# Two attention and MLP layers on one core: Q moved by strided DMAs, stored sums kept in place, and a reordered last stage

## The chip, the core and the metric

The kernel runs on one core of a Trainium2 chip. A core has five engines that run side by side, each through its own list of instructions in order: TensorE (PE, the matmuls; its weight loads are listed as PEld), VectorE (DVE), ScalarE (ACT), GpSimd (POOL) and SyncE (SP, which here only issues DMAs). They wait for each other by semaphores. SBUF is the memory of 128 partitions that all of them use; PSUM is where TensorE puts its results, in 8 banks of 128 x 512 floats. Sixteen DMA engines carry what SP, ScalarE and GpSimd issue.

The metric is the device time of one execution in microseconds (us); smaller is better. Profiles are of one execution, with times counted from the start of its span. Line numbers such as L1420 are lines of the kernel file before the change.

## The reference

```python
def _A_ref(x, wqkv, wo):                      # attention, H = 32 heads of Dh = 16
    qkv = (x @ wqkv).reshape(B, S, 3, H, Dh).transpose(2, 0, 3, 1, 4)
    q, k, v = qkv[0], qkv[1], qkv[2]
    scores = einsum("bhqd,bhkd->bhqk", q, k) * (Dh ** -0.5)
    p = softmax(scores, axis=-1)
    o = einsum("bhqk,bhkd->bhqd", p, v)
    return o.transpose(0, 2, 1, 3).reshape(B, S, D) @ wo
def _B_ref(x, w1, w2):
    return max(x @ w1, 0) @ w2
x = A_x                                       # 1 x 2048 x 512, bf16
x = x + _A_ref(layernorm(x), A_wqkv, A_wo)    # wqkv 512 x 1536, wo 512 x 512
x = x + _B_ref(layernorm(x), B_w1, B_w2)      # w1 512 x 1792, w2 1792 x 512
x = x + _A_ref(layernorm(x), A_wqkv, A_wo)
x = x + _B_ref(layernorm(x), B_w1, B_w2)
```

The same weights serve both layers. The exponentials of the scores are the large part: 2 layers x 32 heads x 2048 x 2048.

## The kernel before, in words

**Tiles and stages.** Queries are cut in four chunks of 512 columns (the second layer's last two chunks are cut further, into three of 256 and two of 128: `chunks`), keys in 16 blocks of 128. The heads are worked in groups: a *run* is one chunk of queries and eight heads (index T, four per layer), and has two *segments*, e = 0 and 1, of four heads each, whose scores stand on four groups of 32 partitions. There are 56 runs, counted through both layers. A *block* is the score of one head's 128 keys against 512 queries (or two or four blocks of keys against 256 or 128 queries). There are 4096 blocks.

**Slots.** The main loop (L1280 to L1446) goes by *slots*. In a slot TensorE scores three blocks into the three banks of one of two PSUM tiles (`ps_s`, L1411), and ScalarE makes one instruction of exponentials over them (L1420). In some slots VectorE takes the third block; ScalarE then has two. Two such blocks make a *pair*, which VectorE turns into exponentials by a chain of its own: `lin` (L1105, from PSUM), two bit masks (`step`, L1146), two products (`cube`, L1157 and L1161), and a scaling (L1158) where V was not scaled beforehand. The result stands as a sum of three terms, so TensorE takes three matmuls with V (L998) for such a block and one for the others. These sums gather in `ps_o`; the ones column of `vaug` gives the softmax denominator in the same matmuls.

**Q.** A run's two heads of a pair share 32 partitions, and the scores of one must not see the other's Q. So Q is kept twice, with the other head's rows set to zero: `q_masked` (L681) has VectorE read the projection from PSUM once per head and multiply by a column of zeros and scales, into `qbuf`, two buffers used by turns. Within the 32 partitions head e = 0 has the first 16, e = 1 the last.

**What ends a segment.** `finish_segment` copies `ps_o` to a buffer `u` (L912), or adds a stored part to it (L910), sends the denominators through small DMAs to a column shape (`c`, L917), inverts them (L939), sends them back (L940), spreads them (a DMA by GpSimd, L942, or a shuffle on VectorE, L952) into a buffer `r` and multiplies (`ot`, L928). There are three `u` and three `r`, taken by turns: segment n waits until segment n - 3 has multiplied. At the start of each layer the keys aren't all there, so partial sums are *stored* (L889, L891) in memory that is free then (`acc0`, in the place of `ht`; `acc`, in that of the first layer's keys and values), and added in the last part.

**The order.** It is written out by the program itself before it is built: a plan keeps a clock for TensorE, VectorE and ScalarE with assumed costs, and puts the projections, the MLP and the layernorms as pieces between the scores where the clocks leave room. `mark` notes when something is made, with a lag where a DMA makes it; `run_until` forces what is missing. VectorE takes a block of a segment up to two segments ahead if that segment's Q is marked and its chain will be done in time. So a change of an assumed cost moves instructions throughout. On the chip each engine follows the order so written, and waits at semaphores.

**Start.** SP and ScalarE load x and the weights; `wqkv` comes in three parts of 512 KB (K on SP; Q, then V on ScalarE), then the rest of x, `wo` and `w2` on SP. The first layernorm, the transposes on TensorE, and the first K, Q and V follow. The later chunks' normed rows are transposed by DMAs on SP (L573); GpSimd does the layernorm's small steps (`ln_seed`, L492 to L500).

**End.** The last chunk has 128 rows. After the last exponential the MLP pieces that are left are run (`run_all`, L1451), among them five groups of the first MLP projection of the chunk before. Then come the last rows' output projection (L1473), layernorm with VectorE steps for the root (`ln_root`), the second projection of the chunk before (`half_part`), and the last rows' MLP, in which the second projection follows the first by one block of 128 features.

Of the kernel before, what the change touches and what calls it, by code (L numbers as in the profile page):

```python
# [19 lines left out]
EPS = 1e-5  # L20
# [5 lines left out]
def kernel(  # L26
# [56 lines left out]
    RSTD_LAG = 4000.0  # L83
    AHEAD = (8.0, 8.0)
# [11 lines left out]
    FULL = 3  # L96

# [11 lines left out]
    wqkv = sb([P, NDC, 3 * D], BF16, "wqkv")  # L109
# [69 lines left out]
    def load_w(engine, a):  # L179
        engine.dma_start(out=wqkv[:, :, a : a + D], in_=wq_src[:, :, a : a + D])  # L180
# [8 lines left out]
    load_w(nc.sync, D)  # L189
    load_w(nc.scalar, 0)  # L190
    load_x(nc.sync, (4, 5, 6, 7))
    load_w(nc.scalar, 2 * D)
    load_x(nc.sync, range(8, NTT))
    nc.sync.dma_start(out=wo[:], in_=A_wo[:, :].rearrange("(c p) f -> p c f", p=P))
    nc.sync.dma_start(out=w2[:], in_=B_w2[:, :].rearrange("(c p) f -> p c f", p=P))

    make_identity(nc, ident[:])
    for kb in range(NKB):
        nc.gpsimd.memset(vaug[0][kb][:, :, DH : DH + 2], 1.0)
    for kb in range(NKB - TPC):  # L200
        nc.gpsimd.memset(vaug[1][kb][:, :, DH : DH + 2], 1.0)


# [6 lines left out]
    def bank():  # L210
        if ending[0]:
            bank_no[0] += 1
            return (ps_f[:], ps_s[0][:, 0, :], ps_s[1][:, 0, :])[bank_no[0] % 3]
# [313 lines left out]

    def ln_apply(tag, tt, i):
        n = ln_n(tag)
        nc.vector.tensor_scalar(  # L530
# [5 lines left out]
    def ln_transpose(tag, i, b=None, at_bank=None):  # L536
        pt = bank().bitcast(BF16) if b is None else b
        for c in range(NDC):
# [3 lines left out]
            if wide[0]:  # L542
                uses(ins, in_bank[0] if b is None else at_bank)
        mark(("xT", tag, i), "pe")
# [5 lines left out]
    def ln_rows(tag, tt, n, i):  # L550
# [10 lines left out]
        if i == n - 1:  # L561
# [6 lines left out]
            def apply(k):  # L568
# [3 lines left out]
                _, l, j = tag  # L572
                nc.sync.dma_start_transpose(  # L573
# [53 lines left out]
    def k_mms(T, j):  # L627
        return [(wqkv[:, c, D + T * P : D + (T + 1) * P], xnT[j][:, c, :]) for c in range(NDC)]
# [11 lines left out]
    def v_mms(kb):  # L640
        j, i = divmod(kb, TPC)
        return [
            (xnT[j][:, c, i * P : (i + 1) * P], wqkv[:, c, 2 * D : 3 * D]) for c in range(NDC)
# [30 lines left out]
    def q_mms(l, j, T):  # L674
        xj, a, w = columns(l, j)
        return [
            (wqkv[:, c, T * P : (T + 1) * P], xnT[xj][:, c, a : a + w]) for c in range(NDC)
# [9 lines left out]
    def q_group(n, l, j, T):  # L687
        xj, _, w = columns(l, j)
        cost = 90 + 2.09 * w

        def fin(b):
            q_masked(n, b, w)
            mark(("q", n))
# [186 lines left out]
    sums_wait = [0]  # L880

    def finish_segment(sg, last):
# [16 lines left out]
        if n >= NU:  # L899
            run_until(("m", n - NU))  # L900
        u, r, c = ubuf[n % NU], rbuf[n % NU], cbuf[n % NU]
# [281 lines left out]
    for e in range(2):  # L1183
# [4 lines left out]
        )  # L1188
        nc.vector.tensor_scalar(
            out=qmask[:, e : e + 1], in0=mask[e], scalar1=SCALE * LOG2E * UNIT, scalar2=None,  # L1190
# [26 lines left out]
    uses(nc.scalar.copy(out=ktp[0][0][0][:], in_=b), in_bank[0])  # L1217
    mark(("k", 0, 0, 0))
# [355 lines left out]
```

## Time and profile before

| | |
|---|---|
| median of 9 runs | 1584.86 us (1582.22 to 1592.49) |
| the profiled execution | 1585.49 us, span 1583.5 us |
| exponentials on ScalarE | 669 over three blocks, 696 over two, one over one |
| pairs on VectorE | 348 |
| Q tiles | 56: 36 of 512 columns, 12 of 256, 8 of 128 |
| first exponential starts, last ends | 14.57 and 1560.85 us |

A group's row in the profile gives line, engine, operation, output and inputs, the number of instructions, the busy time in us, the mean of one in ns, and the idle time of its engine just before it with what ended it. Busy times of one engine can overlap where instructions are pipelined. In a timeline a row gives the start, the length, the instruction, and in brackets the idle time before it. The rows of stretches give start and end, then for each engine the busy time and the number of instructions, then the TensorE clock, the share of the DMA engines and GB/s.

### The profile page before, as it was taken

How to read it: one execution, taken by the hardware profiler on the slowest of the kernel's cores; microseconds unless marked ns; L12 is line 12 of the kernel's file. 1: busy time of each engine (PE TensorE's matmuls, PEld its weight loads, DVE VectorE, ACT ScalarE, POOL GpSimd, SP SyncE). 2: the span in 40 equal slices, each digit the busy share in tenths (PEclk: the TensorE clock that was granted, in tenths of full speed). 3: DMA queues.
4: the chain of work that ended last, by engine and by line, in shares of the span. 5: the costliest groups of instructions: out<-in, count | busy, mean ns of one | idle time of the engine just before them, and what ended most of it. 6: DMA issues, size and time to landing. Idle time of an engine off the chain costs nothing.

```text
span 1583.5 us, 48356 instructions
## 1 busy us (share of the span) xinstructions
PE 1434.3 (91%) x21311; PEld 552.9 (35%) x21311; DVE 1502.4 (95%) x2947; ACT 1549.4 (98%) x1387; POOL 95.8 (6%) x243
## 2 busy tenths in 40 slices
PE   8888889999999989999899998888999999999898
PEld 3222223322332222333233223222334444545665
DVE  7899999999999999999899999999999999999885
ACT  6999999999999999999999999999999999999995
POOL 2000001001010010000100000001001000010000
PEclk9999999998999999999999999999999999999999
DMA  7001100111002120120101000000210211212130
GB/s 193 15 2 26 19 9 18 42 26 25 6 18 43 26 29 6 21 53 11 27 2 27 22 2 1 3 4 9 59 21 17 43 33 27 60 26 58 20 73 16
DMA packets 130145, 44.98 MB, mean 28 GB/s; under 512 B 119280, under 2 KB 127216, under 8 KB 129936
## 3 DMA queue, kind: packets, MB, share of 16 engines
q1 hardware_dynamic: 116864, 29.37, 8.9%
q0 software_dynamic: 11728, 11.23, 4.0%
q8 instruction: 166, 2.72, 0.7%
q10 hardware_dynamic: 1344, 1.31, 0.2%
q14 instruction: 43, 0.35, 0.1%
HBM read 24.38 MB, written 2.10 MB: 17 GB/s over the span
## 4 chain that ended last, share of the span: by engine, by line
ACT 79%; PE 11%; DVE 7%; issue 2%; DMA 1%; ACTq 0%; DVEq 0%
ACT e L1420 79%; PE ps_s L1411 4%; PE ps_o L998 3%; PE ps_f L446 3%; DVE lin L1105 2%; DVE step L1146 1%; DVE cube L1161 1%; DVE cube L1157 1%; DMA wqkv<-in_A_wqkv_dram 1%; PE ps_s L1473 1%; DVE ht L744 0%; DVE q L681 0%; DVE ot L928 0%; DVE u L912 0%; DVE x L705 0%
## 5 line engine op out<-in xcount | busy, mean ns | idle before, releaser
L1420 ACT ACTIVATE e<-ps_s 128x1024 bf16<-128x1024 f32 (+1 forms) x1366 | 1540.1, 1358 | 8.4 <-PE ps_s L1411 7.8
L1411 PE MATMUL ps_s<-q,ktp 32*128 32x512 bf16 (+2 forms) x6699 | 609.6, 325 | 111.9 <-ACT e L1420 101.3
L998 PE MATMUL ps_o<-e,vaug 128*32 128x512 bf16 (+2 forms) x4682 | 497.7, 329 | 8.7 <-DVE u L912 2.7
L1105 DVE TENSOR_SCALAR lin<-ps_s 128x512 int16<-128x512 f32 x696 | 474.3, 684 | 25.3 <-PE ps_s L1411 19.7
L1411 PEld LDWEIGHTS <-ktp 32*128 32x128 bf16 x6699 | 208.9, 91 | 560.9 <-issue 411.7
L998 PEld LDWEIGHTS <-vaug 128*32 128x32 bf16 x6644 | 176.4, 95 | 291.8 <-issue 267.0
L1146 DVE TENSOR_SCALAR step<-lin 128x1024 int16<-128x1024 int16 x696 | 272.7, 416 | 2.1 <-PE ps_o L998 1.2
L1157 DVE TENSOR_TENSOR cube<-step 128x1024 f16<-128x1024 bf16 x348 | 235.4, 681 | 1.7 <-PE ps_f L446 0.5
L1161 DVE TENSOR_TENSOR cube<-cube,lin 128x1024 bf16<-128x1024 f16 x348 | 235.5, 678 | 0.0
L998 PE MATMUL ps_o<-step,vaug 128*32 128x512 bf16 (+2 forms) x950 | 160.0, 328 | 0.0
L446 PE MATMUL ps_f<-w,ht 128*32 128x512 bf16 x1680 | 152.0, 381 | 1.2 <-DVE ht L744 0.5
L446 PE MATMUL ps_f<-xnT,w 128*32 128x512 bf16 (+2 forms) x2080 | 148.2, 341 | 4.7 <-DVE ht L744 3.1
L998 PE MATMUL ps_o<-cube,vthird 128*32 128x512 bf16 (+2 forms) x888 | 143.9, 327 | 0.0
L998 PE MATMUL ps_o<-lin,vaug 128*32 128x512 bf16 (+2 forms) x950 | 126.1, 328 | 6.1 <-DVE u L912 3.7
L446 PE MATMUL ps_f<-xnT,wqkv 128*32 128x512 bf16 (+2 forms) x1376 | 107.8, 351 | 5.4 <-DVE ht L744 1.1
L942 POOL DMA_DIRECT2D r<-u x53 | 39.4, 743 | 1079.9 <-DVE lin L1105 420.0
L446 PE MATMUL ps_f<-wo,ot 128*32 128x512 bf16 x992 | 88.0, 381 | 1.3 <-DVE x L705 1.0
L744 DVE TENSOR_SCALAR ht<-ps_f 128x512 bf16<-128x512 f32 (+1 forms) x107 | 72.7, 679 | 3.3 <-PE ps_f L446 2.7
L446 PEld LDWEIGHTS <-w 128*32 128x32 bf16 x2080 | 59.3, 96 | 34.2 <-issue 17.6
L681 DVE TENSOR_TENSOR q<-ps_f,masks 128x1024 bf16<-128x1024 f32 (+2 forms) x55 | 54.2, 985 | 8.2 <-PE ps_f L446 6.2
L446 PEld LDWEIGHTS <-ht 128*32 128x32 bf16 x1680 | 48.8, 96 | 28.5 <-issue 12.8
L998 PEld LDWEIGHTS <-vthird 128*32 128x32 bf16 x888 | 44.2, 96 | 29.1 <-issue 24.1
(106 smaller groups left out, 609.7 us busy)
## 6 DMA issues: line engine op xcount, KB each, us to landing
w<-in_B_w_dram SPq DMA_DIRECT2D x130, 128.0 KB
r<-u POOLq DMA_DIRECT2D x32, 256.0 KB, 7.4
r<-u POOLq DMA_DIRECT2D x21, 128.0 KB, 4.9
out_dram<-x SPq DMA_DIRECT2D x16, 128.0 KB
x<-in_A_x_dram SPq DMA_DIRECT2D x14, 128.0 KB
w<-in_B_w_dram SPq DMA_DIRECT2D x1, 1792.0 KB
ktp<-in_B_w_dram SPq DMA_DIRECT2D x10, 128.0 KB
wqkv<-in_A_wqkv_dram ACTq DMA_DIRECT2D x2, 512.0 KB
```

Source lines behind the costliest of these rows:

```text
L446: nc.tensor.matmul(out[cols], lhsT[:, cols], rhs, start=i % k == 0, stop=i % k == k - 1, tile_position=(0, 32 * g), skip_group_check=True,)
L681: return nc.vector.tensor_mul(out=qbuf[n % 2][:, :, 0:w], in0=b.rearrange("p (e q) -> p e q", e=1).to_broadcast((P, 2, w)), in1=qmask.rear ...
L744: nc.vector.tensor_scalar(out=out, in0=sums, scalar1=0.0, scalar2=None, op0=ALU.max)
L942: nc.gpsimd.dma_start(out=r[:, 0:width], in_=bass.AP(tensor=sums.tensor, offset=sums.offset, ap=[list(sums.ap[0]), [0, 32], [1, width]],),)
L998: nc.tensor.matmul(ps_o[32 * g : 32 * g + 32, 0 : sg["w"]], values[:, 4 * sg["T"] + g, 2 * e : 2 * e + 32], rhs, start=g not in sg["begun" ...
L1105: first = nc.vector.tensor_scalar(out=lin[which][:, half * QS : (half + 1) * QS], in0=src, scalar1=EXP_BIAS, scalar2=0.0, op0=ALU.add, op1 ...
L1146: nc.vector.tensor_scalar(out=stair, in0=line, scalar1=keep, scalar2=put, op0=ALU.bitwise_and, op1=ALU.bitwise_or,)
L1157: (609, lambda: nc.vector.tensor_mul(out=power, in0=mantissa, in1=mantissa)),
L1161: (609, lambda: nc.vector.tensor_mul(out=power.bitcast(BF16), in0=power, in1=line.bitcast(BF16))),
L1411: nc.tensor.matmul(b[:, a : a + sg["w"]], kt[32 * g : 32 * g + 32, kc : kc + P], qbuf[sg["n"] % 2][32 * g : 32 * g + 32, sg["e"], 0 : sg[" ...
L1420: ex = nc.scalar.activation(out=eb[:, 0 : place[m]], in_=b[:, 0 : place[m]], func=ACTF.Exp, scale=1.0 / (LOG2E * UNIT),)
L1473: uses(nc.tensor.matmul(out, lhsT, rhs, start=first, stop=last), b, needs=needs)
```

## The change

There are four edits, in one program.

1. **Q.** The columns of the K and Q weights are re-sorted, so that within 32 partitions the two heads alternate: e = 0 has the even partitions, e = 1 the odd ones. To do that, the K and Q weights are loaded in eight parts of 128 KB into the memory of `w2`, and copied with a stride into `wkq`, by ScalarE for T = 0 and 1 and by GpSimd for T = 2 and 3. V's weights get their own tile, the load of `w2` is issued after those copies, and `qbuf[1]` is cleared. `q_group` then has two ways. If at least nine slots of work remain before the run and no normed rows wait in `xnbuf[3]`, VectorE evicts Q once, scaled, into `xnbuf[3]`, and two DMAs on SP put the even and odd partitions in place; the plan counts on them 6000 ns later. Else it is the masked copy of before.
2. **Stored sums.** Where a segment has a stored part, the addition writes into the stored part's own memory instead of `u`; all six `u` and `r` buffers become one ring, from which each segment takes what it needs.
3. **Last stage.** VectorE's open tasks are done first, then the output projection and the layernorm of the last rows, and only then what is left of the MLP pieces, on two PSUM banks instead of three. The root is a power on GpSimd. `half_part` is cut in two, with the last rows' transposes between; its result is copied and sent from within the last loop.
4. **Last loop.** The second projection follows the first by three blocks (`LOOK`), not one.

```diff
+    Q_LAG, Q_SLOTS = 6000.0, 9
+    LOOK = 3
-    wqkv = sb([P, NDC, 3 * D], BF16, "wqkv")
+    wkq = sb([P, 2, 4, NDC, P], BF16, "wkq")
+    wv = sb([P, NDC, D], BF16, "wv")
...
+    stage = w2[:].rearrange("p a f -> p (a f)")[:, 0 : 2 * 4 * NDC * P].rearrange(
+        "p (k t c f) -> p k t c f", k=2, t=4, c=NDC
+    )
+    def load_w(engine, k, T):
+        a = (1 - k) * D + T * P
+        engine.dma_start(out=stage[:, k, T], in_=wq_src[:, :, a : a + P])
+    def interleave(copy, k, T):
+        copy(
+            out=wkq[:, k, T].rearrange("p c (g d e) -> p (c g) e d", g=4, e=2),
+            in_=stage[:, k, T].rearrange("p c (g e d) -> p (c g) e d", g=4, e=2),
+        )
...
-    load_w(nc.sync, D)
-    load_w(nc.scalar, 0)
+    load_w(nc.sync, 0, 0)
+    load_w(nc.scalar, 1, 0)
     load_x(nc.sync, (4, 5, 6, 7))
-    load_w(nc.scalar, 2 * D)
+    nc.scalar.dma_start(out=wv[:], in_=wq_src[:, :, 2 * D : 3 * D])
+    for k in range(2):
+        interleave(nc.scalar.copy, k, 0)
     load_x(nc.sync, range(8, NTT))
+    for T in range(2, 4):
+        for k in range(2):
+            load_w(nc.sync, k, T)
     nc.sync.dma_start(out=wo[:], in_=A_wo[:, :].rearrange("(c p) f -> p c f", p=P))
-    nc.sync.dma_start(out=w2[:], in_=B_w2[:, :].rearrange("(c p) f -> p c f", p=P))
     make_identity(nc, ident[:])
+    nc.gpsimd.memset(qbuf[1][:], 0.0)
+    for k in range(2):
+        load_w(nc.gpsimd, k, 1)
...
+    for T in range(2, 4):
+        for k in range(2):
+            interleave(nc.gpsimd.tensor_copy, k, T)
...
     uses(nc.scalar.copy(out=ktp[0][0][0][:], in_=b), in_bank[0])
+    for k in range(2):
+        interleave(nc.scalar.copy, k, 1)
+    nc.sync.dma_start(out=w2[:], in_=B_w2[:, :].rearrange("(c p) f -> p c f", p=P))
...
-        cost = 90 + 2.09 * w
+        cost = 77 + 1.045 * w
         def fin(b):
-            q_masked(n, b, w)
-            mark(("q", n))
+            slots_left = sum(x["left"] * x["w"] for x in segs if x["n"] < n) / (QS * W)
+            if xn_waits[0] or slots_left < Q_SLOTS:
+                q_masked(n, b, w)
+                now_dve[0] += 13 + 1.045 * w
+                mark(("q", n))
+                return
+            qraw = xnbuf[TPC - 1]
+            nc.vector.tensor_scalar(
+                out=qraw[:, 0:w], in0=b, scalar1=SCALE * LOG2E * UNIT, scalar2=None, op0=ALU.mult
+            )
+            for e in range(2):
+                nc.sync.dma_start(out=qbuf[n % 2][e:P:2, e, 0:w], in_=qraw[e:P:2, 0:w])
+            mark(("q", n), lag=Q_LAG)
...
+    ring = deque((x, None) for us in zip(ubuf, rbuf) for x in us)
...
         if n >= NU:
-            run_until(("m", n - NU))
-        u, r, c = ubuf[n % NU], rbuf[n % NU], cbuf[n % NU]
+            run_until(("r", n - NU))
+        c = cbuf[n % NU]
+        def room():
+            buf, of = ring.popleft()
+            if of is not None:
+                run_until(("m", of))
+            ring.append((buf, n))
+            return buf
+        u = room() if sg["load"] is None else sg["load"]
+        r = room()
...
+        nc.vector.tensor_reduce(
+            out=qmask[:, e : e + 1],
+            in_=ident[:].rearrange("p (g d e) -> p e g d", g=4, e=2)[:, e],
+            op=ALU.add, axis=mybir.AxisListType.XY,
+        )
...
-    ending[0] = True
-    run_all()
-    assert not w1_to_load
-    ending[0], wide[0] = False, True
+    while True:
+        t = next((t for t in dve_q if at(t["deps"], "dve") is not None), None)
+        if t is None:
+            break
+        do_task(t)
...
-    ln_root(tag, n_rows)
+    for i in rows:
+        nc.vector.bn_aggr(out=mv[n_last][:, i, :], in_=stats[n_last][:, i, :])
+    nc.vector.tensor_scalar(... op0=ALU.add)
+    nc.gpsimd.tensor_tensor(... op=ALU.pow)
     for i in rows:
         ln_apply(tag, tt + i, i)
+    ending[0] = True
+    run_all()
+    assert not w1_to_load
+    ending[0], wide[0] = False, True
...
-    half_part(0, range(NF))
+    half_part(0, range(NF // 2))
     for i in rows:
         pt = ln_transpose(tag, i, at_bank(more[i]).bitcast(BF16), more[i])
...
+    half_part(0, range(NF // 2, NF))
...
-    for ft in range(NF + 1):
+    for ft in range(NF + LOOK):
+        if ft == NF // 2:
+            for b, x, row in outs:
+                uses(nc.scalar.copy(out=x, in_=at_bank(b)), b)
+                nc.sync.dma_start(out=out_flat[row * P : (row + 1) * P, :], in_=x)
...
-        if ft:
+        if ft >= LOOK:
```

In the order of the changed program's instructions there are 33 Q tiles by DMA (21 of 512 columns, 11 of 256, one of 128), 23 masked ones, 352 pairs, and again 1366 instructions of exponentials.

## The prediction

> **What bounds the kernel now.** I read busy time first, then the chain that ended last, the groups with their shapes kept apart, the stretches by time, and the first and last 25 us instruction by instruction.
>
> ```profile
> span 1583.5 us, 48356 instructions
> PE 1434.3 (91%) x21311; PEld 552.9 (35%) x21311; DVE 1502.4 (95%) x2947; ACT 1549.4 (98%) x1387; POOL 95.8 (6%) x243
> ...
> ACT 79%; PE 11%; DVE 7%; issue 2%; DMA 1%; ACTq 0%; DVEq 0%
> ```
>
> ScalarE is busy 98% of the span and carries 79% of the chain: the exponentials set the time, VectorE (95%) is close behind. By shape:
>
> ```profile
> L1420 ACT ACTIVATE e<-ps_s 128x1536 bf16<-128x1536 f32 x669 | 1009.5, 1572 | 7.0 <-PE ps_s L1411 6.7 <-PE ps_o L998 0.3
> L1420 ACT ACTIVATE e<-ps_s 128x1024 bf16<-128x1024 f32 x696 | 751.5, 1153 | 1.4 <-PE ps_s L1411 1.2
> L1105 DVE TENSOR_SCALAR lin<-ps_s 128x512 int16<-128x512 f32 x696 | 474.3, 684 | 25.3 <-PE ps_s L1411 19.7
> L681 DVE TENSOR_TENSOR q<-ps_f,masks 128x1024 bf16<-128x1024 f32 x35 | 42.6, 1218 | 5.5 <-PE ps_f L446 5.4
> L681 DVE TENSOR_TENSOR q<-ps_f,masks 128x512 bf16<-128x512 f32 x12 | 8.2, 684 | 0.5 <-PE ps_f L446 0.3
> L744 DVE TENSOR_SCALAR ht<-ps_f 128x256 bf16<-128x256 f32 x2 | 0.8, 420 | 0.8 <-PE ps_f L446 0.8
> ```
>
> See two things. ACT idled only 8.4 us in front of its 1366 exponentials. And a slot with two blocks costs 419 ns less than one with three (1572 - 1153): whatever lets VectorE take one more block gives ScalarE 0.419 us. The last stage is bound otherwise:
>
> ```profile
> 1500.00:1560.85 60.85, 55.53 (x1891) 38.17 (x1894) 53.45 (x138) 58.65 (x50) 3.53 (x9) 1.00 0.28 61
> 1560.85:1583.50 22.65, 17.82 (x296) 11.50 (x285) 6.36 (x23) 6.20 (x16) 0.00 (x0) 0.93 0.04 13
> ```
>
> (Columns: TensorE, weight loads, VectorE, ScalarE, GpSimd busy; clock; DMA.) After the last exponential, at 1560.85, TensorE is busy 17.8 of 22.7 us and the others 6: it is a chain with holes.
>
> **The change part by part.**
>
> *Q by DMA.* A Q tile is evicted by VectorE as two masked copies, 1218 ns at 512 columns. In the changed program's order of instructions 33 of 56 become one unmasked eviction (priced by the scores' eviction, 684 ns at 512; 420 at 256) and two strided transfers on SP: 21 of 512 columns, 11 of 256, one of 128. VectorE is freed of 21 x 0.534 + 11 x 0.264 = 14.1 us. The same order has 352 pairs for 348: 8 more first steps (684 ns), 8 more masks (416), 4 x 2 products (about 680), 2 extra scalings (417) = 15.0 us. VectorE's load stays; 8 blocks leave ScalarE: 8 x 0.419 = **-3.35 us**, the slots staying 1366. At worst, if VectorE falls behind, nothing. TensorE adds 16 sum matmuls and drops 15 repeats of scores: nothing, since ScalarE's exponentials cover it.
>
> *The price of Q by DMA.* The transfer must land before TensorE's first score with it, and TensorE stands in order: scores, sums and MLP work wait behind. The code allows it from 9 slots ahead, but VectorE's far blocks may use a Q as soon as it is marked. Counting exponentials between eviction and first use: Q of run 36 has one slot, run 45 four, run 44 five; the other 30 have 8 or more. The trace has no such transfer; its neighbours (an issue on SP; SP's wait for its landing, us in total, times, longest; a broadcast on GpSimd's queue, us from issue to landing):
>
> ```profile
> L917 SPq DMA_DIRECT2D c<-u x86: 540/557/1515, 111.4 to 1551.3; - x86
> SPq L940 <- DMA c<-u: 77.9, 60, 4.0
> r<-u POOLq DMA_DIRECT2D x32, 256.0 KB, 7.4
> ```
>
> Lower bound of the landing L after eviction: 0.1 + two issues of 0.557 + SP's mean wait for such a landing, 77.9/60 = 1.3: 2.5 us. Upper: 7.4 (four times the bytes, GpSimd's queue). I take 3.2, near the first row, same queue and kind, plus 0.7 for two 128 KB weight loads issued just ahead in run 36's case. Its Q was ready at 1158.55 of the trace; an eviction shorter by 0.26 ends at 1158.28; landing, the slot's remaining matmuls and the next three scores (about 0.95) must beat the exponential due at about 1160.75. So the stall is L - 1.5 for one slot, and 1.128 us (1540.1/1366) less for every further slot: L - 4.9 for four, L - 6.0 for five. At L = 3.2: **+1.7**; at 2.5: +1.0; at 7.4: 5.9 + 2.5 + 1.4 = +9.8; nothing if scheduling on the chip runs later.
> [...]
>
> SP's queue gets 66 more issues (37 us); its in-order waits stand behind VectorE and TensorE instructions that precede them in the plan, and the sums' transfers behind them have slack of several slots: nothing; with L as above if not.
>
> *Sums in place.* 20 additions that wrote u write their own source now: same instruction, 680 ns. Shuffles, products and 53 broadcasts keep their number. Nothing, covered by their being unchanged; a buffer freed later or earlier moves VectorE work within its 5% of idle.
>
> *Head.*
>
> ```profile
> 11.85 0.58 ACT L1217 CAST ktp<-ps_s 128x512 bf16<-128x512 f32 x1 [1.88 <-PE ps_s L1212]
> 13.18 1.02 PE L1212 MATMUL ps_f<-wqkv,xnT 128*128 128x512 bf16 x4 [0.50 <-DMA wqkv<-in_A_wqkv_dram]
> 14.57 1.45 ACT L1420 ACTIVATE e<-ps_s 128x1536 bf16<-128x1536 f32 x1 [2.14 <-PE ps_s L1411]
> 18.30 1.05 POOL L500 TENSOR_TENSOR ya<-va,masks 128x4 f32<-128x4 f32 x1
> 22.65 1.38 DVE L530 TENSOR_SCALAR xn<-x,mv,ya 128x512 bf16<-128x512 bf16 x4
> ```
>
> K and Q weights are re-sorted on chip. ScalarE gets four copies (0.59 each by its 128x512 copy): two before 8.90, where it idled 5.7 us; two after 12.43, over by 13.6, before the first exponential at 14.57. The V weights come behind 128 KB instead of 512 KB on their queue, so the 0.50 wait goes, but the first scores still wait for Q's masks, done at 13.95: zero for the first exponential; of the 0.38 us before the second I take half, **-0.2** (0 to -0.4). VectorE's two more reductions (0.22) end before its stats begin at 3.43. GpSimd clears q1, issues two loads, then makes four copies of 128x512 before its layernorm steps (3.1 us, done at 19.35; VectorE wants them at 22.65, so 3.3 us of cover). A copy is 0.2 (its 128x4 steps) to 1.16 us (four times the 0.29 of the 128x128 mask select): 0.8 to 4.6 in all; four like ScalarE's make 2.4. Their loads stand behind SP's x loads, whose last issue ended at 13.96, and take four issues of 0.43 and the 2.0 of L: they land by 17.7, and some 3 earlier if the x loads, one of which waited for V, go sooner (Q and V, 1 MB, took from 3.4 to 13.1; 0.64 MB would take 6). Copies and layernorm then end at 20.2 to 23.2: hidden for the most part, and I take zero. The second-projection weights, formerly issued at 14.48, now wait on SP for all these copies; behind them stand the transposes of the next rows, issued at 23.80, whose K groups TensorE runs at about 38. Cover some 4 us; beyond it VectorE, TensorE and ScalarE stall one for one: 0 to +4.
> [...]
>
> *Tail.*
>
> ```profile
> 1563.44 0.35 DVE L964 SCALAR_TENSOR_TENSOR ot<-ps_o,masks,r 128x128 bf16<-128x128 f32 x1
> 1565.56 1.89 PE L1473 MATMUL ps_s<-wo,ot 128*128 128x512 bf16 x8
> 1572.32 0.61 PE L1473 MATMUL ps_s<-xnT,w 128*128 128x128 bf16 x8 [0.46 <-ACT xnT L1513]
> 1580.05 0.58 ACT L1540 CAST x<-ps_s 128x512 bf16<-128x512 f32 x1 [0.53 <-PE ps_s L1473]
> ```
>
> Before, TensorE does 160 small MLP matmuls (1561.5 to 1565.3) ahead of the output projection, then waits twice. After: seven projection matmuls from 1561.9, the eighth at 1563.98 when ot is there; the 160 (3.54 us) to 1567.8, 0.2 more for two banks instead of three; half the other row block's sums (8 x 0.213) to 1569.7, its load and product on SP and ScalarE moved into the loop; transposes 0.2; the second half 1.5, to 1571.4; the residual 0.2. The layernorm runs beside this: copy, stats 0.69, two small steps, power on GpSimd (0.82 by its 128x2 row) for eight VectorE steps of 0.19, done at 1567.7, 2 us early. The loop: before 7.65 us, a block every 0.50; looking ahead three blocks, TensorE alone counts, 4 x 0.056 + 0.213 = 0.437, 14 blocks 6.1. End of sums 1577.8 for 1579.97: **-2.1** (-2.6 without bank waits; -1.2 if the loop keeps 0.50).
>
> **Sum.** -3.35 + 1.7 - 0.2 - 2.1 = -3.95 us. The profiled execution took 1585.49 (span 1583.5 plus 2.0 outside) and becomes 1581.5; it lies 0.63 above the median of 1584.86, so the median becomes **1580.9**.
>
> **Rivals.**
> - *Q transfers cost nothing*: VectorE or TensorE run later than planned and L hides; the eviction and the use are one slot apart, against it. -3.35 - 0.4 - 2.6: 1578.5.
> - *Head*: copies or the weight load arrive late, the transposes with them. For it: VectorE, TensorE and ScalarE are all in order there. +4: 1584.9.
> - *The gain on ScalarE is not taken* (VectorE at 95% falls behind): no -3.35: 1584.3.
> - *Slower: Q late behind the weight loads*. Four loads in a row took SP 3.78 us (0.95 each); ten stand ahead of run 45's Q. With L = 9 the three stalls are 7.5 + 4.1 + 3.0 = 14.6 instead of 1.7: 1593.8. It turns the change into a loss from L = 6.0 (4.5 + 1.1 + 0 = 5.6), into one of over 0.3% from 7.6. Against it: SP mostly waits for VectorE in this trace.
>
> **How the numbers follow.** A measurement tells 0.3%, 4.75 us, from no change. Chances: forecast 0.43 (1578.5 to 1583.5), free transfers 0.23, head 0.15, gain not taken 0.08, slower 0.11. Faster means under 1580.1: the second case and half the first, 0.44. Slower, over 1589.6: the last, 0.11. The rest 0.45. The range takes the free case with a better head, 1576.5, and up to the head case with late Qs, 1588; the forecast alone 1578.5 to 1583.5.
>
> **What would show it.** 661 exponentials of 1536 and 704 of 1024; a hole of 1 to 2 us in ScalarE near 1155, released by TensorE waiting for a q transfer, and little elsewhere; the first exponential still at 14.5; from the last exponential to the end of the span 20.6 us for 22.65. I am wrong if q transfers hold TensorE in many places, if VectorE waits for GpSimd at 20 to 25 us, or if the tail's loop keeps its 0.50.

## The result and the profile after

| | before | changed |
|---|---|---|
| median | 1586.85 us (1580.96 to 1593.09) | 1580.42 us (1576.97 to 1584.05) |
| ratio, 95% interval | | 0.996 (0.995 to 0.9971) |
| profiled execution: time, span | 1585.49, 1583.5 us | 1581.73, 1579.9 us |
| first exponential starts, last ends, last copy starts | 14.57, 1560.85, 1580.05 | 14.42, 1560.75, 1576.34 |

The changed kernel is faster by 0.40% (0.29 to 0.50), 6.4 us by the medians; the two profiled spans differ by 3.6. The page of the changed kernel, busy times and the chain:

```profile
span 1579.9 us, 48434 instructions
PE 1435.7 (91%) x21255; PEld 548.5 (35%) x21255; DVE 1498.9 (95%) x2967; ACT 1549.3 (98%) x1391; POOL 107.6 (7%) x251
...
ACT 76%; PE 11%; DVE 9%; issue 3%; DMA 0%; ACTq 0%; DVEq 0%
```

ScalarE still sets the end, 98% busy. Its groups by shape in the changed kernel:

```profile
L1481 ACT ACTIVATE e<-ps_s 128x1536 bf16<-128x1536 f32 x661 | 1000.8, 1576 | 4.4 <-PE ps_s L1472 3.7 <-PE ps_o L1051 0.3
L1481 ACT ACTIVATE e<-ps_s 128x1024 bf16<-128x1024 f32 x704 | 761.3, 1156 | 4.9 <-PE ps_s L1472 4.7
```

The counts are those predicted, 661 and 704. But the busy time of all 1366 fell by 2.6 us only (1540.1 to 1537.5), and the stretch from the first exponential's start to the last one's end didn't shrink: 1546.33 us for 1546.28. What was gained in busy time went into idle time, mostly in four places. One of them is the wait that was predicted for run 36. TensorE's waits, ScalarE around that place, and the stretches of 3.41 us there (columns: TensorE, weight loads, VectorE, ScalarE, GpSimd busy; clock; DMA), all of the changed kernel:

```profile
PE ps_s L1472 <- DMA q<-xn: 1.3, 1, 1.3
```

```profile
1161.70 1.02 ACT L1481 ACTIVATE e<-ps_s 128x1024 bf16<-128x1024 f32 x1 [1.22 <-PE ps_s L1472]
1163.16 1.45 ACT L1481 ACTIVATE e<-ps_s 128x1536 bf16<-128x1536 f32 x1 [0.44 <-PE ps_s L1472]
```

```profile
1154.87:1158.29 3.42, 3.41 (x56) 1.45 (x55) 3.42 (x9) 3.42 (x4) 0.00 (x0) 1.00 0.15 31
1158.29:1161.70 3.41, 1.68 (x21) 0.54 (x23) 1.95 (x5) 2.19 (x3) 0.68 (x1) 1.00 0.21 47
1161.70:1165.11 3.41, 3.41 (x28) 0.70 (x24) 2.15 (x5) 2.47 (x2) 0.00 (x0) 0.50 0.30 49
1165.11:1168.52 3.41, 3.41 (x50) 1.13 (x49) 3.10 (x7) 3.10 (x3) 0.00 (x0) 1.00 0.21 34
```

It is the one wait for a Q transfer in the whole kernel. Follow the clock: TensorE waits 1.33 us, so it is busy 1.68 of 3.41 us, and the next 3.41 us it is granted half its clock. Two more holes of ScalarE follow, 0.44 and 0.81: the transfer cost 1.22 by its wait and 1.25 by what the wait did to the clock.

The other three places are like it without a transfer: 3.4 us from 175.3 and 6.8 us each from 578.1 and 1045.7 at clock 0.50, with 1.0, 1.3 and 1.7 us of ScalarE's idle time. Before, there was one such place in the loop (10.2 us from 383.0, 2.2 us idle) and another at the start of the last stage, in these stretches of the kernel before:

```profile
1557.19:1560.60 3.41, 2.30 (x82) 1.85 (x84) 1.82 (x7) 3.41 (x4) 0.00 (x0) 1.00 0.02 5
1560.60:1564.01 3.41, 3.41 (x140) 3.41 (x130) 1.61 (x4) 0.81 (x3) 0.00 (x0) 0.50 0.02 5
```

The last stage of the changed kernel runs at full clock throughout (stretches by time, and ScalarE in the last stage):

```profile
1500.00:1560.75 60.75, 56.38 (x1934) 39.47 (x1926) 55.86 (x144) 59.54 (x51) 2.77 (x9) 1.00 0.28 61
1560.75:1579.90 19.15, 15.38 (x270) 9.73 (x269) 5.08 (x15) 6.08 (x16) 0.56 (x1) 1.00 0.05 16
```

```profile
1563.57 0.59 ACT L1545 CAST x<-ps_s 128x512 bf16<-128x512 f32 x1 [2.82 <-PE ps_s L1535]
...
1576.34 0.58 ACT L1619 CAST x<-ps_s 128x512 bf16<-128x512 f32 x1 [0.63 <-PE ps_s L1535]
```

From the last exponential's end to the last copy it takes 15.6 us for 19.2. So this pair of profiles puts the gain in the last stage, and the main loop comes out even.

### The profile page after: what moved, and what is told of

The parts are those of the page before. It is cut to its first block, busy times and chain, and to the rows that moved or that the text cites. A ratio compares the mean times of both kernels' runs of the same rounds, so it can differ in the third digit from the quotient of the medians.

```text
span 1579.9 us, 48434 instructions
## 1 busy us (share of the span) xinstructions
PE 1435.7 (91%) x21255; PEld 548.5 (35%) x21255; DVE 1498.9 (95%) x2967; ACT 1549.3 (98%) x1391; POOL 107.6 (7%) x251
## 4 chain that ended last, share of the span: by engine, by line
ACT 76%; PE 11%; DVE 9%; issue 3%; DMA 0%; ACTq 0%; DVEq 0%
ACT e L1481 76%; PE ps_s L1472 4%; PE ps_f L472 3%; PE ps_o L1051 3%; DVE lin L1158 2%; DVE step L1199 1%; DVE cube L1210 1%; DVE cube L1214 1%; DVE ht L786 1%; PE ps_s L1535 1%; DVE q L712 0%; DVE stats L509 0%; DVE u L965 0%; DVE ot L981 0%; DVE x L747 0%
## 5 line engine op out<-in xcount | busy, mean ns | idle before, releaser
L1481 ACT ACTIVATE e<-ps_s 128x1024 bf16<-128x1024 f32 (+1 forms) x1366 | 1537.5, 1359 | 9.6 <-PE ps_s L1472 8.6
L1051 PE MATMUL ps_o<-e,vaug 128*32 128x512 bf16 (+2 forms) x4666 | 503.6, 329 | 10.9 <-DVE u L965 5.4
L1472 PEld LDWEIGHTS <-ktp 32*128 32x128 bf16 x6611 | 204.0, 92 | 555.1 <-issue 407.8
L1051 PEld LDWEIGHTS <-vaug 128*32 128x32 bf16 x6676 | 181.7, 94 | 297.4 <-issue 273.5
L1199 DVE TENSOR_SCALAR step<-lin 128x1024 int16<-128x1024 int16 x704 | 276.6, 417 | 1.1 <-PE ps_o L1051 0.4
L1051 PE MATMUL ps_o<-cube,vthird 128*32 128x512 bf16 (+2 forms) x888 | 148.7, 327 | 0.0
L472 PE MATMUL ps_f<-xnT,wkq 128*32 128x512 bf16 (+2 forms) x1376 | 107.3, 354 | 4.5 <-DVE ht L786 1.0
L995 POOL DMA_DIRECT2D r<-u x46 | 33.0, 717 | 922.4 <-DVE step L1199 302.3
L472 PEld LDWEIGHTS <-wkq 128*32 128x32 bf16 x1376 | 37.6, 96 | 29.2 <-issue 17.0
```

The source lines that it names most:

```text
L472: nc.tensor.matmul(out[cols], lhsT[:, cols], rhs, start=i % k == 0, stop=i % k == k - 1, tile_position=(0, 32 * g), skip_group_check=True,)
L995: nc.gpsimd.dma_start(out=r[:, 0:width], in_=bass.AP(tensor=sums.tensor, offset=sums.offset, ap=[list(sums.ap[0]), [0, 32], [1, width]],),)
L1051: nc.tensor.matmul(ps_o[32 * g : 32 * g + 32, 0 : sg["w"]], values[:, 4 * sg["T"] + g, 2 * e : 2 * e + 32], rhs, start=g not in sg["begun" ...
L1199: nc.vector.tensor_scalar(out=stair, in0=line, scalar1=keep, scalar2=put, op0=ALU.bitwise_and, op1=ALU.bitwise_or,)
L1472: nc.tensor.matmul(b[:, a : a + sg["w"]], kt[32 * g : 32 * g + 32, kc : kc + P], qbuf[sg["n"] % 2][32 * g : 32 * g + 32, sg["e"], 0 : sg[" ...
L1481: ex = nc.scalar.activation(out=eb[:, 0 : place[m]], in_=b[:, 0 : place[m]], func=ACTF.Exp, scale=1.0 / (LOG2E * UNIT),)
```

## The experiments

All kernels were timed in turn with the kernel before on the same chip, in three batches; the batch of a kernel decides which runs its ratio refers to. "Idle" is the time from the first exponential's start to the last one's end less their busy time, "tail" the time from there to the start of the last copy, both of the one profiled execution. With the start of the first exponential and the 3.3 to 4.0 us from the start of the last copy to the end, busy, idle and tail add up to the span. "Clock" is the granted clock of that execution; the last two columns use all executions of a kernel and are explained below the table.

| kernel | 1536s | Qs by DMA | median us | ratio (95%) | clock | busy | idle | tail | mean clock, all | at full clock |
|---|---|---|---|---|---|---|---|---|---|---|
| before | 669 | 0 | 1586.85 | 1 | 0.996 | 1540.1 | 6.2 | 19.2 | 0.9943 | 1581.4 |
| changed | 661 | 33 | 1580.42 | 0.9960 (0.9950-0.9971) | 0.994 | 1537.5 | 8.9 | 15.6 | 0.9940 | 1575.4 |
| e_tail | 669 | 0 | 1581.22 | 0.9958 (0.9945-0.9972) | 0.997 | 1539.7 | 4.8 | 16.7 | 0.9976 | 1579.4 |
| e_no_tail | 661 | 33 | 1581.51 | 0.9966 (0.9954-0.9977) | 0.990 | 1537.8 | 9.3 | 18.4 | 0.9939 | 1577.4 |
| e_all_masked | 671 | 0 | 1581.44 | 0.9969 (0.9952-0.9986) | 0.995 | 1540.7 | 6.5 | 14.5 | 0.9952 | 1578.5 |
| e_no36 | 663 | 34 | 1578.64 | 0.9947 (0.9931-0.9963) | 0.997 | 1538.1 | 5.9 | 14.5 | 0.9950 | 1575.3 |
| e_floor60 | 663 | 35 | 1576.65 | 0.9937 (0.9917-0.9958) | 1.000 | 1537.9 | 4.1 | 14.1 | 1.0000 | 1576.3 |
| e_floor50 | 663 | 36 | 1590.51 | 1.0044 (1.0018-1.0069) | 0.983 | 1539.9 | 17.5 | 14.9 | 0.9816 | 1576.1 |
| e_early_q | 661 | 46 | 1609.66 | 1.0141 (1.0116-1.0166) | 0.975 | 1541.4 | 40.4 | 15.0 | 0.9825 | 1594.2 |
| e_look1 | 661 | 33 | 1580.82 | 0.9964 (0.9948-0.9980) | 0.988 | 1538.4 | 10.9 | 16.9 | 0.9937 | 1575.5 |
| e_before60 | 667 | 0 | 1587.79 | 1.0007 (0.9992-1.0021) | 0.999 | 1540.2 | 7.1 | 16.3 | 0.9958 | 1583.3 |
| e_tail60 | 667 | 0 | 1582.03 | 0.9976 (0.9960-0.9992) | 0.998 | 1540.4 | 8.2 | 14.4 | 0.9975 | 1580.5 |
| e_no_tail60 | 663 | 35 | 1580.58 | 0.9969 (0.9953-0.9984) | 0.999 | 1538.1 | 4.2 | 15.4 | 0.9979 | 1579.0 |
| e_masked60 | 667 | 0 | 1580.51 | 0.9969 (0.9953-0.9986) | 1.000 | 1539.8 | 4.4 | 14.9 | 0.9983 | 1579.5 |

The record has the granted clock of every execution, and the time follows it. Lost clock is the span times what the clock lacks of 1. One slope for all fourteen kernels, 0.56 us of time for each us of lost clock, leaves the 222 executions (81 of them of the kernel before, from the three batches) 0.9 us off their lines (standard deviation) and gives each kernel a time at full clock. This is a fit, good to about 1 us: the clocks are on record to 0.001 only, e_look1 should stand above the changed kernel by the 1.3 us that its trace shows and doesn't, and e_before60 fits badly (a slope of its own would be 0.86 and give 1581.2).

The theory after the result was: the terms of the sum are about right, the wait at run 36 costs more through the clock, and the stretches at half clock, which fall differently in each execution, make up the rest. The rivals were that one part is worth far more than said, or that the clock has no hand in it. For the medians the table speaks against the last part of the theory: the kernels before and after the change both have a mean clock of 0.994, so the stretches cost both some 5 us, and at full clock 6.0 us are left between them.

### The last stage alone: e_tail

The kernel before with edits 3 and 4 (in the diff of the change: `LOOK`, `bank`, and all from the open tasks of VectorE to the end).

> The kernel before with the last stage's edits alone (order of the output projection, half of the other rows' sums, power on GpSimd, three blocks ahead). The plan up to the last exponential is that of before: 669 exponentials of 1536. Theory (the tail term, -2.1, was right and the -3.6 seen between the two profiled executions holds 1.5 us in which TensorE ran at half clock in one of them by chance): the time falls by 2.1 us, 0.13%, and this trace has 19.2 - 2.1 = 17.1 us from the last exponential's end to the start of the last copy if TensorE drops to half clock there, 15.6 if it does not. Rival (the term was too small, the order itself is worth 3.6): 3.6 us, 0.23%, and the clock stays full there because of the order.

Measured: 0.42% faster, 7 us (4 to 9), more than either. The trace is smaller than the clock: the tail is 16.7 us at full clock against 19.2, 2.5 less with the same plan up to the last exponential; ScalarE's idle time in the loop is 1.4 less, though that part of the program is the same, with two stretches of 3.4 us at half clock for one of 10.2. By the two traces the order is worth more than the 2.1 of the prediction. Most of the rest of the 7 us is in the clocks on record: 0.9976 on the mean of the five executions of e_tail, 0.9931 on that of the 23 of the kernel before in the same batch, which is worth 4 us by the line. Since the plan up to the last exponential is the same, most of these 4 us are more likely a draw than the edit; that isn't shown.

### All but the last stage: e_no_tail

The changed kernel with `LOOK`, `bank` and the last stage as before.

> The changed kernel with the last stage of before: Q by DMA, stored sums in place and the new head. 661 exponentials of 1536, as in the changed kernel. Theory: -3.35 for eight blocks, -0.4 at the head, +2.5 for the one wait for a Q transfer with the half clock behind it: -1.3 us against before, 0.08%. Rival 1 (the wait costs its 1.2 us alone): -2.5. Rival 2 (the last stage is worth 2.1 and all the rest of the 6.4 us comes from here): -4.3, 0.27%. A hole of 1.2 us in ScalarE in front of run 36, as in the changed kernel, in all of them; in theory TensorE is at half clock behind it again.

Measured: 5.4 us faster (3.6 to 7.3); the theory's -1.3 missed, the second rival's -4.3 lies inside. Its profiled execution, at 1586.2 us, is far above its own median: it had 17 us at half clock from 750.7 (2.8 us of idle time) and 6.8 from 1047.7. What it shows well is the two things that were to be told apart. Its old tail at full clock takes 18.4 us where the changed kernel, with the same plan before it, takes 15.6: -2.8. And the wait at run 36 came again, with half the clock behind it. Its stretches of 3.41 us there:

```profile
1156.97:1160.39 3.42, 3.41 (x53) 1.38 (x52) 3.42 (x9) 3.42 (x4) 0.00 (x0) 1.00 0.18 37
1160.39:1163.80 3.41, 1.99 (x26) 0.61 (x23) 2.27 (x6) 2.50 (x3) 0.68 (x1) 0.99 0.19 45
1163.80:1167.21 3.41, 3.41 (x32) 0.80 (x24) 1.91 (x5) 2.23 (x2) 0.00 (x0) 0.51 0.29 47
```

So it did in the trace of e_look1, the third with this plan. ScalarE's holes there were 1.22, 0.44 and 0.81 us; 0.91, 0.27 and 0.92; 1.04, 0.50 and 0.74: 2.3 us on the mean, 1.06 of it the wait itself.

### No Q by DMA: e_all_masked

```diff
-    Q_LAG, Q_SLOTS = 6000.0, 9
+    Q_LAG, Q_SLOTS = 6000.0, 1e9
```

> The changed kernel with no Q by DMA: all 56 evicted in two masked copies, the rest as changed. 671 exponentials of 1536 (two more than before, ten more than changed). Theory: against before +0.8 for the two blocks, -0.4 at the head, -2.1 to -3.6 in the tail: -1.7 to -3.2, so it is 3 to 5 us slower than the changed kernel if VectorE's relief counts in full, less 2.5 for the wait that it does not have: 1 to 3 us slower. Rival (Q by DMA gives nothing net): the same time as the changed kernel or up to 1 us faster.

Measured: 4.9 us faster than before (2.2 to 7.6); the changed kernel's interval and its own overlap (0.9950 to 0.9971, 0.9952 to 0.9986). By these ratios Q by DMA, as it stands in the changed kernel, is not told from nothing: ten blocks on one side, the wait with its half clock on the other. At full clock, where the half clock behind the wait doesn't count, it is worth 3.1 us by the table, give or take 1, and 3.2 between e_masked60 and e_floor60.

### The one near Q masked: e_no36

```diff
-            if xn_waits[0] or slots_left < Q_SLOTS:
+            if xn_waits[0] or slots_left < Q_SLOTS or n == 36:
```

> The changed kernel with the Q of run 36 evicted by masked copies, as before; 34 others go by DMA, none nearer than three slots to its first use. 663 exponentials of 1536 instead of 661. Theory: the hole of 1.22 us and the two behind it (0.44 and 0.81, TensorE at half clock) go, two blocks come back at 0.42: 2.5 - 0.8 = 1.6 us faster than the changed kernel. Rival (the half clock behind the wait was chance, or VectorE's time was the limit there): 1.2 - 0.8 = 0.4 us faster, or no difference. No wait of TensorE for a Q transfer above 0.3 us is expected in either.

Measured: 0.9947 for 0.9960, 2 us faster than the changed kernel by the ratios, as said, but with intervals that overlap. The trace is clear: no wait of TensorE for a Q is left, and no stretch at half clock near 1160. ScalarE's wait for scores, all in all, in e_no36:

```profile
ACT e L1481 <- PE ps_s L1472: 5.6, 15, 0.8
```

In the changed kernel it was 8.6, with 1.22 as the longest.

### More and less work for TensorE: e_floor60, e_floor50

The plan repeats scores where TensorE would have little to do. One constant sets how much it must have.

```diff
-    FLOOR = 0.56
+    FLOOR = 0.60
```

and 0.50 in the other kernel.

> The changed kernel with the floor for TensorE's work, which the plan keeps by repeating scores, raised from 0.56 to 0.60. 663 exponentials of 1536, 347 repeats (the changed kernel has 661 and 279; the run without the near Q 663 and 289). Of the Qs by DMA one stands two slots before its first use, the others three and more. Theory (the spread above some 1576 us is stretches of 3.4 us at half clock, which follow stretches in which TensorE did little, each worth 0.9 us): with more repeats there are fewer of them: two or three for the five or six of the changed kernel, 1577.5 to 1579. Rival (the stretches have nothing to do with TensorE's work, or the repeats themselves hold up ScalarE): as many stretches as in the changed kernel, 1580 to 1582.

> The same with the floor lowered to 0.50: 663 exponentials of 1536, 100 repeats. One Q (of run 37) one slot before its first use. Theory: many more stretches at half clock, granted clock 0.98 or less for 0.994, and at 0.525 us of time for each us of lost clock 1588 or more. Rival: the stretches come by chance whatever TensorE does: 1580 to 1583, clock 0.994.

Measured: 1576.65 us with no stretch at half clock between the first exponential and the last copy (clock 1.00), and 1590.51 with nine such places, 55 us in all (clock 0.983). 347 repeats against 100, the same 663 exponentials. ScalarE's groups, first of e_floor60, then of e_floor50:

```profile
L1481 ACT ACTIVATE e<-ps_s 128x1536 bf16<-128x1536 f32 x663 | 998.0, 1568 | 3.7 <-PE ps_s L1472 2.7 <-PE ps_o L1051 0.5
L1481 ACT ACTIVATE e<-ps_s 128x1024 bf16<-128x1024 f32 x702 | 754.0, 1150 | 1.1 <-PE ps_s L1472 0.8
```

```profile
L1481 ACT ACTIVATE e<-ps_s 128x1536 bf16<-128x1536 f32 x663 | 1014.1, 1591 | 9.9 <-PE ps_s L1472 8.6 <-PE ps_o L1051 0.7
L1481 ACT ACTIVATE e<-ps_s 128x1024 bf16<-128x1024 f32 x702 | 768.1, 1175 | 8.3 <-PE ps_s L1472 8.1
```

The idle time in front of the exponentials is 4.8 against 18.2 us. The theory held for e_floor50 (1588 or more) and said a little too much for e_floor60 (1577.5 to 1579). The trace of e_floor50 has other waits too: two Qs are waited for (2.3 us), and VectorE waits for the transfers of two others (1.5). But at full clock the table has the two kernels within its error, 1576.3 and 1576.1, so the 14 us between them are clock, as far as the fit can tell. e_floor60 is the fastest kernel of this study, 10 us under the kernel before; against the changed kernel the intervals just overlap.

### Q by DMA from seven slots ahead: e_early_q

```diff
-    Q_LAG, Q_SLOTS = 6000.0, 9
+    Q_LAG, Q_SLOTS = 6000.0, 7
```

> The changed kernel with Q by DMA allowed from seven slots ahead instead of nine: 46 Qs by DMA for 33, 661 exponentials of 1536 as before, 303 repeats. Eight Qs (two of 512 columns, one of 256, five of 128) are evicted one slot before their first use, one two slots, three three slots; in the changed kernel it is one. Theory (landing of the transfers 2.2 to 2.4 us after the end of the eviction, and a TensorE that has waited drops to half clock): 1.2 us for each plus about 1.2 for the half clock, seven more than in the changed kernel: 7 x 2.5 = +17 us against the changed kernel, some 1598. Rival 1 (the half clock behind run 36 was chance): 7 x 1.2 = +8, some 1589. Rival 2 (it mostly hides, run 36 is an exception): within 3 us of the changed kernel.

Measured: 29 us slower than the changed kernel, more than the theory's 17. Three waits of e_early_q:

```profile
PE ps_s L1472 <- DMA q<-xn: 12.2, 7, 3.1
DVE xn L559 <- DMA q<-xn: 7.9, 3, 4.1
ACT e L1481 <- PE ps_s L1472: 33.7, 45, 3.5
```

Seven waits of TensorE, 1.7 us each. The second row was in no expectation: the Q to be moved stands in a buffer of normed rows, and VectorE may not write the next rows there until the transfers have read it; that took 7.9 us, once 4.1. TensorE was at half clock for 82 us, against 20 in the changed kernel. Behind five of the seven waits half clock began within 2.4 us; those that ended at 94.9 and 1487.1 had not. Of the 29 us the line gives 10 to the lower clock and leaves 19. Here the distance to the first use decides whether a transfer is hidden.

### The last loop one block ahead: e_look1

```diff
-    LOOK = 3
+    LOOK = 1
```

> The changed kernel with the last loop one block ahead instead of three; all else as changed. Theory: the loop's block goes back from 0.437 to 0.50 us, 14 x 0.063 = +0.9 us at the least; with the two blocks that no longer wait at its start +1.2: from the copy of x behind the output projection to the last copy 13.7 to 14.0 us for 12.77. Rival (the gain of the tail was the order alone): no difference in the trace from copy to copy. The medians can't tell this apart; the trace can.

Measured: from the copy of x to the last copy 14.10 us for 12.77. ScalarE in the last stage of e_look1:

```profile
1566.46 0.58 ACT L1545 CAST x<-ps_s 128x512 bf16<-128x512 f32 x1 [2.82 <-PE ps_s L1535]
...
1577.76 0.28 ACT L1604 ACTIVATE ht<-ps_s 128x128 bf16<-128x128 f32 x1 [0.72 <-PE ps_s L1535]
1578.76 0.28 ACT L1604 ACTIVATE ht<-ps_o 128x128 bf16<-128x128 f32 x1 [0.72 <-PE ps_o L1535]
...
1580.56 0.59 ACT L1619 CAST x<-ps_s 128x512 bf16<-128x512 f32 x1 [0.53 <-PE ps_s L1535]
```

That is just above the theory's 13.7 to 14.0. Two blocks come every 1.00 us; three ahead, the same rows of the changed kernel are 0.875 apart. The look-ahead is 1.3 of the tail's 2.8 us.

### The parts with the higher floor: e_before60, e_tail60, e_no_tail60, e_masked60

Each is the kernel named with `FLOOR = 0.60`: the kernel before, e_tail, e_no_tail and e_all_masked.

> The kernel before with the floor for TensorE's work raised from 0.56 to 0.60 and nothing else: 667 exponentials of 1536 (before 669), 345 repeats. The run of the changed kernel with this floor took 1576.65 at a clock of 1.00. Theory: at full clock the change is worth four blocks at 0.43, 0.3 at the head and 2.8 in the tail, 4.8 us together, so this run takes 1581.4, and raising the floor alone gives the kernel before some 5 us, 0.3%. Rival (the change works through fewer stretches at half clock, and its own terms are worth less): under 1579.

> The kernel before with the floor at 0.60 and the last stage's edits: 667 exponentials of 1536, 345 repeats, the plan of the run with the floor alone up to the last exponential. Theory: 2.5 to 2.8 us less than that run, 1578.6 to 1578.9, and 2 us above the changed kernel with this floor. Rival (the order of the last stage is worth the predicted 2.1 or less): 1579.3 or more.

> The changed kernel with the floor at 0.60 and the last stage of before: 663 exponentials of 1536, 347 repeats, 35 Qs by DMA. Theory: 2.5 to 2.8 us above the changed kernel with this floor, 1579.2 to 1579.5, and 2 us (four blocks at 0.43 and 0.3 at the head) below the kernel before with this floor. Rival (Q by DMA gives nothing net): the same as the kernel before with this floor.

> The changed kernel with the floor at 0.60 and no Q by DMA: 667 exponentials of 1536, 349 repeats. Theory: four blocks more than the changed kernel with this floor, +1.7 us: 1578.3; less 0.3 at the head it is the run of the last stage's edits alone with this floor. Rival 1 (transfers still cost some us even where none is near): the same as the changed kernel with this floor or faster. Rival 2 (VectorE's masked copies hold up more than the count of blocks says): 1580 or more.

Measured: raising the floor gave the kernel before nothing (1.0007), against the theory's 5 us and the rival's more. In e_before60 the clock hardly rose: ten of its twelve executions had 0.995 or 0.996, where all six of e_floor60 had 1.000. e_tail60 and e_masked60 came out in the ranges of their rivals (1579.3 or more; 1580 or more), and e_no_tail60, at 1580.58, a good 1 us above its theory and far from its rival. Against e_before60, the last stage is worth 0.31%, the rest 0.38%, both together (e_floor60, from another batch) 0.70%, so at this floor the ratios add up; they contain the clocks, though, which go from 0.9958 to 1.0000 over these kernels, some 4 us of the 0.70%. e_masked60 stands 0.32% above e_floor60. The profiled spans of e_before60 and e_floor60, 1581.5 and 1573.5, add up as follows: 0.3 at the first exponential, 2.3 in busy time (four blocks, predicted 1.7), 3.0 in idle time, 2.3 in the tail. Of the idle time 1.0 is a stretch at half clock (at 111). Two of the others are in e_before60 and, to the hundredth, in e_tail60, which has the same plan. ScalarE in e_before60, then in e_tail60:

```profile
1169.00 122.27 ACT L1420 ACTIVATE e<-ps_s 128x1536 bf16<-128x1536 f32 x108 [0.68 <-PE ps_s L1411]
1309.54 41.60 ACT L1420 ACTIVATE e<-ps_s 128x1536 bf16<-128x1536 f32 x37 [0.95 <-PE ps_s L1411]
```

```profile
1169.74 122.27 ACT L1421 ACTIVATE e<-ps_s 128x1536 bf16<-128x1536 f32 x108 [0.68 <-PE ps_s L1412]
1310.28 40.68 ACT L1421 ACTIVATE e<-ps_s 128x1536 bf16<-128x1536 f32 x36 [0.95 <-PE ps_s L1412]
```

These two holes come with the plan, and an edit of the main loop makes another plan; e_masked60 has none there. They are a term of 1 to 2 us that no part of the change owns.

e_before60's median lies 4.3 us above its profiled execution. The clocks say why: the profiled one had 0.999, the ten executions at 0.995 and 0.996 took 1585.4 to 1589.1 us, the two at 0.998 and 0.999 took 1583.5. So the spans above are from the fast end of e_before60. Why the higher floor raised the clock to 1.000 in the changed kernel and not in the kernel before is open.

## Why the prediction was right or wrong

The time was right (1580.9, measured 1580.42), and so was the side. Against the median of before that belongs to the same measurement the gain is 6.4 us (4.6 to 7.9), where the sum said 3.95. That the time fits to 0.5 us is in part luck: the sum started from a base 2.0 us below that median, and its gain was 2.5 us too small. By its steps:

- **Q by DMA, -3.35: the mechanism right, the size not settled.** The counts came as said. Busy time of the exponentials in the three executions with the plan of the changed kernel: 1537.5, 1537.8 and 1538.4; in the two with that of before: 1540.1 and 1539.7. That is -2.0 for eight blocks, 0.25 a block for the 0.419 of the two rows. Other pairs in the table give more: 0.32 (e_all_masked and changed, ten blocks), 0.48 (e_masked60 and e_floor60, four) and 0.58 (e_before60 and e_floor60, four). The instructions over three blocks became longer by 1 to 5 ns; why wasn't settled.
- **Price of Q by DMA, +1.7: the place right, a part missing.** One wait, at run 36, none at 44 and 45, which need L above 4.9. L was 2.3 (the eviction ended at 1158.98, the first score with that Q ran at 1161.29), below the 2.5 given as its lower bound. The wait cost 1.22 in this trace, where L - 1.5 gives 0.8, and 1.06 on the mean of three. The step that failed is the line "So the stall is L - 1.5": it ends when the transfer lands, but TensorE came out of the wait at half clock, which cost another 1.2 each time. Together +2.3. The eviction, the two issues and the first score in the changed kernel:

```profile
1158.57 0.41 DVE L730 TENSOR_SCALAR xn<-ps_f 128x256 bf16<-128x256 f32 x1
1159.00 1.46 SPq L734 DMA_DIRECT2D q<-xn  x2
1161.29 0.37 PE L1472 MATMUL ps_s<-q,ktp 32*128 32x256 bf16 x2 [1.33 <-DMA q<-xn]
```

- **The terms of L.** Of the 3.2 in the sum the rows gave 2.5; the 0.7 on top, for the weight loads, was the author's estimate, which no run shows, and L came out without it. SP issued the pair at run 36 in 1.46 us from 1159.00, where two issues were put at 1.11, and the first score ran 0.83 us after that, where the row's mean wait was 1.3.
- **Sums in place, 0**: no wait of the traces names it, and e_tail60 and e_masked60, which differ by it and the head, have the same 667 exponentials and intervals that overlap. It was not undone alone.
- **Head, -0.2: nothing.** The first exponential starts at 14.2 to 14.6 in four traces with the old head and at 14.2 to 15.0 in ten with the new one. The hole before the second fell from 0.38 to 0.13 in all of the new ones, but also in e_tail and e_tail60, with the old head. The risk of +4 fell: the copies took GpSimd 0.73 us each, and VectorE's step for the normed rows came with no wait. GpSimd, then VectorE, in the changed kernel:

```profile
15.10 2.93 POOL L192 COPY wkq<-w 128x512 bf16<-128x512 bf16 x4 [9.34 <-DMA w<-in_A_wqkv_dram]
20.04 1.07 POOL L526 TENSOR_TENSOR ya<-va,masks 128x4 f32<-128x4 f32 x1
...
22.24 1.37 DVE L559 TENSOR_SCALAR xn<-x,mv,ya 128x512 bf16<-128x512 bf16 x4
```

- **Tail, -2.1: too small by the traces.** At full clock and with five groups of the MLP left over, -2.8. The sum took the 160 small matmuls at 3.54 us from the trace of before, which ran them at half clock for the most part (0.50 from 1560.6 to 1564.0); they took 2.87 in the changed kernel. The fit at full clock has 2.0 for the last stage in both pairs (e_tail and before, changed and e_no_tail), which its error can't tell from either number. The term also depends on what the plan leaves over: -2.8 with five groups, -1.9 with two (e_before60, e_tail60), -1.3 with four matmuls of the 32 of one group (e_no_tail60, e_floor60). In the new order these groups fill TensorE's wait for the layernorm; in the old one they stand ahead of it.
- **The sum.** With the measured sizes, -2.0 + 2.3 + 0 - 2.8 = -2.5 us. The profiled spans gave -3.6, of which 0.8 is the half clock in the old tail (19.2 against 18.4 in e_no_tail). The medians gave -6.4. Between the traces and the medians stands the clock: the changed kernel's profiled execution had 0.994, the one of before 0.996, which is worth 2 us, while all executions have the same mean. Between the sum and the traces stands idle time of which no term speaks. Without all stretches at half clock the pair of traces gives -2.6 in busy time, +1.2 for the wait, -2.8 in the tail and -1.6 in ScalarE's other idle time (4.0 before, 2.4 after), -5.8 together, and the table has 6.0 at full clock. The -1.6 are small holes that no run ties to an edit. The prediction treated the profiled execution as the kernel less 0.63 us. But one execution is one draw of the half-clock stretches, and the median of before itself was 1584.86 over nine runs and 1586.85 over 63: that the base moves by half the sum was no term of it and no rival.
- **Rivals.** Free transfers fell by the one wait; the head by the traces; the gain on ScalarE was taken in part. The slower one (L of 6 and more) was not the case, but e_early_q shows the mechanism it feared, at 29 us, by another route: not a late landing, but an early use.

## What to carry to other kernels

A wait of TensorE can cost more than its length: behind run 36 half clock added 1.2 us to a wait of 1.06 on the mean, three times of three, and in e_early_q it followed five waits of seven. Add what half clock costs afterwards, and read the clock column of the stretches that you take durations from. A transfer in place of VectorE's copy was free here only as far as the first use lay behind it, so count that distance for each one in the order as built; one of 33 was too near, and its 2.3 us stand against the 2.0 of busy time that all of them freed. Before a kernel whose limiting engine is busy 98% of the time is compared by single traces, see how often its clock drops in each, and use the clock of every execution on record.

## What the runs showed of the hardware

- **TensorE's granted clock changed on a grid of 3.413 us.** That is the length of the shortest half-clock stretches in the clock record of the changed kernel's trace. There the half-clock stretches began at 175.3, 578.1, 1045.7 and 1161.7: 118.0, 137.0 and 34.0 times 3.413 apart. In the kernel before, 383.0 and 1560.6 are 345.0 apart. They last 3.4 and 6.8 us in the first trace, 10.2 and 3.4 in the second.
- **TensorE was partly busy before half clock.** In 23 half-clock stretches of nine traces it was busy 49 to 70% of the 3.41 us before, in most cases in several pieces, with waits of 0.2 to 1.3 us between. The share alone doesn't settle it: in the kernel before the 3.41 us from 994.0 were busy 62%, and full clock followed. Three executions of the changed kernel's main loop had half clock at four, four and three places before the last exponential, and only the one behind run 36 is in all three. That the rest is chance, as the plan's places with little work meet the grid or don't, is argued and not shown.
- **What it costs.** Over the 22 recorded executions of the changed kernel the granted clock went from 0.990 to 0.997 and the time from 1584.05 to 1576.97 us. A straight line through them gives 0.52 us for each us of lost clock (correlation 0.89), 0.9 us for a stretch of 3.4, and 1575.7 at full clock; e_floor60, whose profiled execution had full clock, took 1575.35. The 81 recorded executions of the kernel before give 0.55 (correlation 0.96).
